# Attention with a router on one core: the place where token ranks are summed, the order of VectorE's work around the second scan, and idle products at the start

## The chip, the cores and the metric

One program on one core of one Trainium2 chip. The metric is device time in microseconds; runs of the same kernel are compared by their median. TensorE (PE) multiplies, VectorE (DVE), ScalarE (ACT) and GpSimd (POOL) do elementwise work, SyncE (SP) issues most of the transfers. Each engine works through its own queue in order.

## The reference

Gated linear attention (a recurrence over time) gives x; a cosine router sends each token to one of eight experts.

```python
# q, k, v, alpha: (4, 8, 768, 48); w1: (8, 384, 1024); w2: (8, 1024, 384)
for t in range(S):
    state = alpha[:, :, t, :, None] * state + np.einsum('bhd,bhe->bhde', k[:, :, t], v[:, :, t])
    y[:, :, t] = np.einsum('bhd,bhde->bhe', q[:, :, t], state)
x = y.transpose(0, 2, 1, 3).reshape(3072, 384)
logits = (x / norm(x)) @ (emb / norm(emb)).T / tau
e = argmax(logits); gate = softmax(logits)[e]
out = gate * (relu(x @ w1[e]) @ w2[e])
```

## The kernel before

The sequence is cut into 24 chunks of 128 tokens, six to each batch entry. One loop over `s` runs 28 iterations; iteration `s` does a different step for several chunks at once, so that every engine has work:

- `keys_back(s - 1)`: four transposes on PE (`pkb`), not for a batch entry's last chunk. They are the first products of an iteration, and their start is taken below as the iteration's start (`pa` where they are missing).
- `rows(s - 3)`: eight products that turn chunk `s - 3` into token rows with their router logits; VectorE sums the logits (`x`, L605), ScalarE copies the rows (L609).
- `decays(s)`: transposes of decays, keys and queries (`pa`, `pk`, `pq`, L416). VectorE scans `pa` backwards (`r`, L460), makes `kr` (L467), a reciprocal (`ini`, L470) and the second scan, forwards (`a`, L474). GpSimd multiplies the queries by `a` (`qs`, L479).
- `scores(s - 1)`: 16 records of products of `kr` and `qs` (`sc`, L540); VectorE masks one half (`sm`, L543), ScalarE copies the other and GpSimd masks it (L545).
- `mix_states(s - 2)` (L566), `update(s - 1)` (`pd`, L519, into the single bank of the pool `ps_mm`; VectorE adds `dec` to it and gives `state`, L527 or L529), `mix_chunk(s - 2)` (L579).

Every third chunk or so a group of tokens is complete (`GROUPS`). `choose(g)` then finds each token's expert on VectorE (`top`, `win`, `best`, `chosen`) and GpSimd adds the counts (`before`, L322, one addition for each chunk): in the program at the end of iterations 5, 8, 11, 14, 17, 20, 22 and later. One iteration on, in 6, 9, 12, 15, 18, 21, 23 and later, `place(g)` sums the ranks with two small products (L331, L335); VectorE makes row numbers of them (`at_row`, `row`, `dest`), and GpSimd sends one chunk of tokens to memory in each iteration (`xs`, L294), all that are left from iteration 21 on. GpSimd also copies token numbers into the next group's rows (`x` from `toks`, L603), which waits until the transfers out of that buffer have landed.

After the loop come the experts, eight in turn, with PE working throughout. The first expert's early part (`pxe`, `phe`) is in the last iterations, once its weights have come.

The code's order is not the final one: a scheduler lays out each engine's queue from the dependences, and `issue_after` holds an instruction back behind another. A pool's buffers are reused in turn, and a bank must be read before it is written again.

Of the kernel before, what the change touches and what calls it, by code (L numbers as in the profile page):

```python
# [9 lines left out]
FP32 = mybir.dt.float32  # L10
I32 = mybir.dt.int32
AF = mybir.ActivationFunctionType
ALU = mybir.AluOpType
# [14 lines left out]
def kernel(  # L28
# [12 lines left out]
    nc = tc.nc  # L41
    B, H, S, D = q.shape
    E, DM = expert_emb.shape
    F = w1.shape[2]
    P = 128
    DP = 64
    NP = H // 2
    NCH = S // P
    N = B * S
    NS = N // P  # L50
# [15 lines left out]
    S0, EARLY = 18, 2  # L66
# [117 lines left out]
    with ExitStack() as c1:  # L184
# [73 lines left out]
        def prepare_first(a0):  # L258

            p0 = ps_tr.tile([P, NP, NS], FP32, tag="tr", name="p0")  # L260
            for p in range(NP):
                nc.tensor.transpose(
                    p0[:, p], a0[:, 2 * p : 2 * p + 2].rearrange("s h d -> s (h d)"),
                    ident[:NS, :NS],
                )
            nc.vector.tensor_copy(al0, p0)
# [54 lines left out]
                eng = nc.vector if s == NS - 1 else nc.gpsimd  # L321
                eng.tensor_tensor(before[:, s + 1], before[:, s], chosen[:, s], ALU.add)  # L322

        def place(g, pyx):

            s0, s1 = GROUPS[g]
            n = s1 - s0
            ch = chosen[:, s0:s1]
            rkf = pyx[:, 0, RK : RK + n * E]
            rk = rkf.rearrange("p (s e) -> p s e", e=E)  # L330
            nc.tensor.matmul(  # L331
                rkf, lhsT=ones, rhs=before[:, s0:s1].rearrange("p s e -> p (s e)"),
                start=True, stop=False, skip_group_check=True,
            )
            nc.tensor.matmul(  # L335
                rkf, lhsT=earlier, rhs=ch.rearrange("p s e -> p (s e)"),
                start=False, stop=True, skip_group_check=True,
            )
            at = work.tile([P, GMAX, E], FP32, name="at_row")[:, 0:n]
            nc.vector.tensor_tensor(at, rk, ch, ALU.mult)  # L340
            row = work.tile([P, GMAX], FP32, name="row")[:, 0:n]
            nc.vector.tensor_reduce(row.unsqueeze(2), at, axis=AX.X, op=ALU.add)
            nc.vector.tensor_copy(dest[:, s0:s1], row)
            send.extend(range(s0, s1))
# [68 lines left out]
        def turned(t, name):  # L413
            pt = ps_tr.tile([P, NP * P], FP32, tag="tr", name=name)
            for p in range(NP):
                nc.tensor.transpose(  # L416
                    pt[:, p * P : (p + 1) * P],
                    t[:, 2 * p : 2 * p + 2].rearrange("p h d -> p (h d)"),
                    ident,
                )  # L420
            return pt
# [17 lines left out]
        def behind(s):  # L439

            queue = ExitStack()
            for call in st[s]["last"]:
                queue.enter_context(tc.issue_after(call.ins))
            return queue

        def decays(s):

            c = s % NCH
            d = st[s]
            i = s % NBUF
            L = NP * P
            pa = turned(at_s[i], "pa")
            r = r_s[s % NR]
            nc.vector.tensor_tensor_scan(  # L460
                r[:, L - 2 :: -1], pa[:, L - 1 : 0 : -1], inr[:, L - 2 :: -1],
                1.0, ALU.mult, ALU.add,
            )
            pk = turned(kt_s[i], "pk")
            d["kr"] = kr = work.tile([P, NP, P], FP32, name="kr", bufs=3)
            krf = kr.rearrange("p n t -> p (n t)")
            nc.vector.tensor_tensor(krf, pk, r, ALU.mult)  # L467
            rv = r.rearrange("p (n t) -> p n t", t=P)
            ini = ini_s[s % 2]
            nc.vector.reciprocal(  # L470
                ini.rearrange("p (n t) -> p n t", t=P)[:, :, 0:1], rv[:, :, 0:1]
            )
            a = work.tile([P, L], FP32, name="a")
            by_dve = nc.vector.tensor_tensor_scan(a, pa, ini, 0.0, ALU.mult, ALU.add)  # L474
            pq = turned(qt_s[i], "pq")
            d["qs"] = qs = work.tile([P, NP, P], FP32, name="qs", bufs=4)
            qc = work.tile([P, NP * P], FP32, name="qc")
            nc.scalar.copy(qc, pq)  # L478
            by_pool = nc.gpsimd.tensor_tensor(  # L479
                qs.rearrange("p n t -> p (n t)"), qc, a, ALU.mult  # L480
            )
            if c > 0:
                d["end"] = end = work.tile([P, NP, 1], FP32, name="end", bufs=3)
                nc.gpsimd.tensor_tensor(end, rv[:, :, 0:1], al0[:, :, s : s + 1], ALU.mult)
            d["last"] = by_dve, by_pool
# [22 lines left out]
        def update(s):  # L508

            c = s % NCH  # L510
            if c == NCH - 1:
                return
            d = st[s]
            kb, vt = d["kb"], vt_s[s % NBV]
            pd = ps_mm.tile([P, NP, DP], FP32, tag="mm", name="pd")
            for p in range(NP):
                for hh in range(2):
                    h = 2 * p + hh
                    nc.tensor.matmul(  # L519
                        pd[DP * hh : DP * hh + DP, p],  # L520
                        lhsT=kb[:, h * DP : (h + 1) * DP],
                        rhs=vt[:, h],
                        start=True, stop=True,
                    )
            carried["state"] = state = work.tile([P, NP, DP], FP32, name="state")
            if c == 0:
                nc.vector.tensor_copy(state, pd)  # L527
            else:
                nc.vector.tensor_tensor(state, pd, d["dec"], ALU.add)  # L529

        def scores(s):

# [18 lines left out]

        NQ = NP // 2
        YX = NQ * P
        RK = YX + NQ * (2 * D + E)

        def mix_states(s):
            d = st[s]
# [78 lines left out]
        def warm(n):  # L636

            pw = ps_mm.tile([P, P], FP32, tag="mm", name="pw")
            for _ in range(n):
                nc.tensor.matmul(pw, lhsT=ident, rhs=ident, start=True, stop=True)  # L640
# [8 lines left out]
        for s in range(NS + 4):  # L649
            if s + 2 <= NS:  # L650
                load(s + 2)
            if 0 <= s - 1 < NS:
                keys_back(s - 1)

            r = s - 4
            g = group_of[r] if r >= 0 else 0
            due = r >= 0 and r == GROUPS[g][1] - 1
            if 0 <= s - 3 < NS:
                rows(s - 3)
                if due:  # L660
                    place(g, st[s - 3]["pyx"])
            elif due:
                place(g, ps_y.tile([P, 2, 512], FP32, name="pyx"))
            if s < NS:
                decays(s)
            if s == 0:
                with behind(s):
                    prepare_first(a0)
                warm(2)
            if 0 <= s - 1 < NS:  # L670
                decay_state(s - 1)
                scores(s - 1)
# [1 line left out]
                mix_states(s - 2)  # L674
            if 0 <= s - 1 < NS:
                update(s - 1)
            if 0 <= s - 2 < NS:
                mix_chunk(s - 2)
            if s == 1:
# [14 lines left out]
                first_layer_early(0, 2)  # L694
            if s == NS + 1:
                first_layer_early(2, 4)
            if r == S0 - 1:
                first_expert()
            with behind(s) if s < NS else ExitStack():
                for c in send[:] if s >= S0 + 3 else send[:1]:  # L700
                    to_rows(dest[:, c : c + 1], x_g[group_of[c]][:, c - GROUPS[group_of[c]][0]])
# [266 lines left out]
```

## Time and profile before

| | us |
|---|---|
| median of 3 runs | 477.31 (474.83 to 478.24) |
| the profiled execution | 473.6 |
| its span, first to last instruction | 471.8 |

1.8 us of the profiled execution lie outside the span. PE is busy for 445.9 us of the span (95%) at a mean granted clock of 0.973; VectorE, ScalarE and GpSimd are busy for 37, 31 and 29%. Times in the trace are microseconds from the span's start. The granted clock is 1.00 at 2.4 GHz and 0.50 at 1.2 GHz. A busy figure for PE holds modelled ends, so an idle time is read from the waits, not from 100% less the busy share.

### The profile page before, as it was taken

The numbers are of one execution on the slowest core, as the hardware profiler recorded it, in microseconds if no ns is written. First come the engines' busy times: TensorE is split into PE (matmuls) and PEld (weight loads), VectorE is DVE, ScalarE is ACT, GpSimd is POOL, SyncE is SP. The second block draws the span as 40 slices with busy tenths as digits, with TensorE's granted clock in tenths as the row PEclk, the third lists the DMA queues.
The fourth block names the chain that finished last, engine by engine and source line by source line (L and its number), as shares of the span: only waits on it lengthen the run. The fifth ranks groups of instructions, "written<-read, shape, count | busy, mean of one in ns | idle before, by whom it ended". The sixth has DMA issues, their size and how long they took to land. (4 is left out here: it accounts for less than half of the span.)

```text
span 471.8 us, 8748 instructions
## 1 busy us (share of the span) xinstructions
PE 445.9 (95%) x3286; PEld 313.0 (66%) x3287; DVE 174.0 (37%) x467; ACT 147.5 (31%) x304; POOL 137.4 (29%) x231
## 2 busy tenths in 40 slices
PE   7899989998998998999999999999999999999993
PEld 6787878787887876676655655555656555655551
DVE  6787476785867752341221111111221121011010
ACT  3343334343334342373640330201650250210200
POOL 6356455655636642430101001010200101001001
PEclk9899889998989899999999999999999999999997
DMA  9999996885862396286702704501901800001000
GB/s 138 163 158 158 173 176 135 152 150 122 167 120 69 100 360 233 68 268 250 273 1 85 293 17 156 196 18 31 322 32 25 329 0 35 16 1 47 1 18 31
DMA packets 119362, 60.02 MB, mean 127 GB/s; under 512 B 102287, under 2 KB 113816, under 8 KB 119312
## 3 DMA queue, kind: packets, MB, share of 16 engines
q1 hardware_dynamic: 115208, 49.14, 44.4%
q0 software_dynamic: 3728, 10.16, 6.0%
q8 instruction: 32, 0.52, 0.5%
q14 instruction: 18, 0.15, 0.1%
q10 hardware_dynamic: 376, 0.05, 0.1%
HBM read 49.69 MB, written 11.45 MB: 130 GB/s over the span
## 5 line engine op out<-in xcount | busy, mean ns | idle before, releaser
L799 PE MATMUL ph<-xT,w 128*128 128x384 f32 (+1 forms) x384 | 119.4, 462 | 1.5 <-ACT hT L803 0.5
L810 PE MATMUL pyo<-w,hT 128*128 128x384 f32 x352 | 115.6, 488 | 0.0
L799 PEld LDWEIGHTS ph<-xT,w 128*128 128x128 f32 x384 | 67.7, 190 | 44.0 <-issue 5.2
L810 PEld LDWEIGHTS pyo<-w,hT 128*128 128x128 f32 x352 | 66.3, 190 | 45.3
L737 POOL DMA_INDIRECT out_dram<-y,sx x25 | 24.1, 965 | 232.0 <-DVE y L813 168.6
L803 ACT ACTIVATE hT<-ph 128x384 f32<-128x384 f32 (+1 forms) x64 | 29.1, 459 | 121.4 <-PE ph L799 121.3
L813 DVE TENSOR_SCALAR y<-pyo,gt 128x384 f32<-128x384 f32 x22 | 13.6, 618 | 108.9 <-PE pyo L810 108.9
L479 POOL TENSOR_TENSOR qs<-qc,a 128x512 f32<-128x512 f32 x24 | 30.5, 1272 | 40.7 <-DVE a L474 21.3
L753 DVE COPY xT<-pxg 128x384 f32<-128x384 f32 (+1 forms) x30 | 15.1, 503 | 66.6 <-PE pxg L752 63.6
L540 PE MATMUL sc<-qs,kr 64*128 64x128 f32 x384 | 31.4, 298 | 1.7 <-DVE en L277 1.5
L460 DVE TENSOR_TENSOR_SCAN r<-pa,inr 128x511 f32<-128x511 f32 x24 | 29.2, 1218 | 4.1 <-PE pa L416 4.1
L540 PEld LDWEIGHTS sc<-qs,kr 64*128 64x128 f32 x384 | 25.6, 196 | 6.4 <-issue 3.6
L474 DVE TENSOR_TENSOR_SCAN a<-pa,ini 128x512 f32<-128x512 f32 x24 | 29.4, 1224 | 1.2 <-DVE ini L470 0.5
L294 POOL DMA_INDIRECT xs<-x,dest x24 | 24.5, 1020 | 14.3 <-ACT ehT L633 5.1
L579 PE MATMUL pyx<-sm,vt 128*64 128x128 f32 x384 | 27.9, 292 | 0.0
L595 PE MATMUL pyx<-sel,yT 128*128 128x104 f32 x192 | 27.0, 284 | 0.2 <-ACT yT L585 0.2
L585 ACT COPY yT<-pyx 128x512 f32<-128x512 f32 x24 | 14.1, 586 | 39.0 <-PE pyx L579 39.0
L595 PEld LDWEIGHTS pyx<-sel,yT 128*128 128x128 f32 x192 | 23.6, 193 | 3.7 <-ACT yT L585 3.3
L579 PEld LDWEIGHTS pyx<-sm,vt 128*64 128x64 f32 x384 | 22.9, 149 | 0.9 <-issue 0.9
L762 ACT ACTIVATE gx<-xg 128x384 f32<-128x384 f32 x32 | 16.7, 522 | 15.8 <-DMA xg<-xs 14.7
L478 ACT COPY qc<-pq 128x512 f32<-128x512 f32 x24 | 14.0, 584 | 23.7 <-PE pq L416 23.3
L609 ACT COPY x<-pyx 128x384 f32<-128x384 f32 x24 | 11.6, 483 | 24.7 <-DVE x L605 24.7
(169 smaller groups left out, 514.7 us busy)
## 6 DMA issues: line engine op xcount, KB each, us to landing
w<-in_moe_w_dram SPq DMA_DIRECT2D x16, 1536.0 KB, 9.6
kt<-in_k_dram SPq DMA_DIRECT2D x24, 192.0 KB, 3.6
qt<-in_q_dram SPq DMA_DIRECT2D x24, 192.0 KB, 5.0
vt<-in_v_dram SPq DMA_DIRECT2D x24, 192.0 KB, 4.0
xg<-xs SPq DMA_DIRECT2D x22, 196.5 KB, 7.6
at<-in_alpha_dram SPq DMA_DIRECT2D x24, 168.0 KB, 4.8
xg<-xs SPq DMA_DIRECT2D x8, 98.2 KB
at<-in_alpha_dram SPq DMA_DIRECT2D x24, 22.5 KB, 4.3
```

Of the source, the lines that this page charges most:

```text
L294: ins = nc.gpsimd.indirect_dma_start(out=xs, out_offset=bass.IndirectOffsetOnAxis(ap=rows, axis=0), in_=x, in_offset=None, bounds_check=E ...
L460: nc.vector.tensor_tensor_scan(r[:, L - 2 :: -1], pa[:, L - 1 : 0 : -1], inr[:, L - 2 :: -1], 1.0, ALU.mult, ALU.add,)
L474: by_dve = nc.vector.tensor_tensor_scan(a, pa, ini, 0.0, ALU.mult, ALU.add)
L479: by_pool = nc.gpsimd.tensor_tensor(qs.rearrange("p n t -> p (n t)"), qc, a, ALU.mult)
L540: nc.tensor.matmul(sc[hh][:, p], lhsT=kr[sl, p], rhs=qs[sl, p], start=True, stop=True)
L579: nc.tensor.matmul(pyx[to : to + DP, hh, q * P : (q + 1) * P], lhsT=vt[:, 2 * p + hh], rhs=sm[hh][:, p], start=("dec" not in d and q == 0) ...
L595: nc.tensor.matmul(px[:, hh, q], lhsT=yT[:, hh, q], rhs=sel[:, hh, q], start=True, stop=True, skip_group_check=True,)
L737: ins = nc.gpsimd.indirect_dma_start(out=out, out_offset=bass.IndirectOffsetOnAxis(ap=col, axis=0), in_=y, in_offset=None, bounds_check=N - 1,
L762: nc.scalar.activation(x2, xg[:, t, 0:DM], AF.Square, accum_out=sq[:, t])
L799: nc.tensor.matmul(ph, lhsT=w1_t[:, i, f * P : (f + 1) * P], rhs=xT[:, i], start=(i == 0), stop=(i == KT - 1),)
L803: nc.scalar.activation(hT[:, f], ph, AF.Relu)
L810: nc.tensor.matmul(py, lhsT=hT[:, f], rhs=w2_t[:, f], start=(f == 0), stop=(f == FT - 1),)
```

## The change

Four edits:

- `place(g)` no longer writes into columns of the bank pair of `pyx`, which `rows` uses, but into a tile `rk` of the pool `ps_mm`, the one bank that `update` writes; and it is called near the end of the iteration, no longer right behind `rows`.
- `decays(s)` is split. Its second half, `decay_queries(s)` (reciprocal, second scan, `qs`, `end`), is called behind `update(s - 1)`, and held back on the queues until VectorE's state sum of chunk `s - 1` where there is one.
- `prepare_first` and its two idle products move with it, still in iteration 0.
- Five idle products (`warm(5)`, tile `pw`, in `ps_mm` too) are called in iteration 1.

On PE, the place of iteration 9 (names: `pyx` and `rk` written from `before` and `chosen` are the ranks; `pyx` from `sel` is `rows`). Before:

```order
L494 MATMUL pkb<-ident,kr 128x128 x4
L416 MATMUL pa<-ident,at_116 128x128 x2
L595 MATMUL pyx<-sel,yT 128x104 x4
L416 MATMUL pa<-ident,at_116 128x128 x2
L416 MATMUL pk<-ident,kt_124 128x128 x4
L416 MATMUL pq<-ident,qt_120 128x128
L331 MATMUL pyx<-before,ones 128x24
L335 MATMUL pyx<-chosen,earlier 128x24
L416 MATMUL pq<-ident,qt_120 128x128 x3
```

and now, from the update of that iteration to the scores of the next:

```order
L525 MATMUL pd<-vt_130,kb 64x64 x8
L584 MATMUL pyx<-sm_944,vt_129 64x128 x4
L584 MATMUL pyx<-sm_945,vt_129 64x128 x4
L331 MATMUL rk<-before,ones 128x24
L335 MATMUL rk<-chosen,earlier 128x24
L500 MATMUL pkb<-ident,kr 128x128 x4
L416 MATMUL pa<-ident,at_117 128x128
L600 MATMUL pyx<-sel,yT 128x104 x4
L416 MATMUL pa<-ident,at_117 128x128 x3
```

The rank products stood among the transposes of the same iteration and now stand behind its last products.

On VectorE, iteration 8, in which a group's experts are chosen. Before:

```order
L460 SCALAR_TENSOR_TENSOR r_134<-pa,inr 128x511
L312 TENSOR_REDUCE top<-x 128x3
L467 TENSOR_TENSOR kr<-pk,r_134 128x512
L470 RECIPROCAL ini_135<-r_134 128x4
L314 TENSOR_TENSOR win<-x,top 128x24
L474 SCALAR_TENSOR_TENSOR a<-pa,ini_135 128x512
L315 TENSOR_TENSOR win<-win,first 128x24
L317 TENSOR_REDUCE best<-win 128x3
L543 TENSOR_TENSOR sm_944<-sc_946,causal 128x512
L319 TENSOR_TENSOR chosen<-win,best 128x24
L529 TENSOR_TENSOR state<-pd,dec 128x256
```

and now:

```order
L459 SCALAR_TENSOR_TENSOR r_134<-pa,inr 128x511
L312 TENSOR_REDUCE top<-x 128x3
L466 TENSOR_TENSOR kr<-pk,r_134 128x512
L314 TENSOR_TENSOR win<-x,top 128x24
L315 TENSOR_TENSOR win<-win,first 128x24
L317 TENSOR_REDUCE best<-win 128x3
L319 TENSOR_TENSOR chosen<-win,best 128x24
L549 TENSOR_TENSOR sm_944<-sc_946,causal 128x512
L535 TENSOR_TENSOR state<-pd,dec 128x256
L479 RECIPROCAL ini_135<-r_134 128x4
L483 SCALAR_TENSOR_TENSOR a<-pa,ini_135 128x512
```

The second scan `a` stood ahead of the mask and the state sum and is now the last of them; `chosen` comes ahead of the mask.

On GpSimd, from the query product of iteration 8 to that of iteration 9. Before:

```order
L479 TENSOR_TENSOR qs<-qc,a 128x512
L688 MEMSET xg_91 128x393
L294 DMA xs<-x,dest 25024x393
L545 AFFINE_SELECT sm_945<-sm_945 128x512
L322 TENSOR_TENSOR before<-before,chosen 128x8
L504 TENSOR_TENSOR dec<-state,end 128x256
L322 TENSOR_TENSOR before<-before,chosen 128x8 x2
L603 COPY x<-toks 128x3
L484 TENSOR_TENSOR end<-r_132,al_139 128x4
L479 TENSOR_TENSOR qs<-qc,a 128x512
```

and now:

```order
L485 TENSOR_TENSOR qs<-qc,a 128x512
L692 MEMSET xg_91 128x393
L294 DMA xs<-x,dest 25024x393
L490 TENSOR_TENSOR end<-r_132,al_139 128x4
L608 COPY x<-toks 128x3
L551 AFFINE_SELECT sm_1046<-sm_1046 128x512
L510 TENSOR_TENSOR dec<-state,end 128x256
L485 TENSOR_TENSOR qs<-qc,a 128x512
```

The count's additions are no longer in this stretch (they now stand ahead of the query product of iteration 8), and the copy of token numbers now stands ahead of a mask and of `dec`.

The diff:

```diff
-        def place(g, pyx):
+        def place(g):
...
-            rkf = pyx[:, 0, RK : RK + n * E]
-            rk = rkf.rearrange("p (s e) -> p s e", e=E)
+            rk = ps_mm.tile([P, GMAX, E], FP32, tag="mm", name="rk")[:, 0:n]
+            rkf = rk.rearrange("p s e -> p (s e)")
             nc.tensor.matmul(
                 rkf, lhsT=ones, rhs=before[:, s0:s1].rearrange("p s e -> p (s e)"),
-                start=True, stop=False, skip_group_check=True,
+                start=True, stop=False,
             )
...
             nc.vector.tensor_tensor(krf, pk, r, ALU.mult)
+            pq = turned(qt_s[i], "pq")
+            d["qc"] = qc = work.tile([P, NP * P], FP32, name="qc")
+            nc.scalar.copy(qc, pq)
+            d["a"] = pa, r
+
+        def decay_queries(s):
+            c = s % NCH
+            d = st[s]
+            L = NP * P
+            pa, r = d["a"]
             rv = r.rearrange("p (n t) -> p n t", t=P)
...
             by_dve = nc.vector.tensor_tensor_scan(a, pa, ini, 0.0, ALU.mult, ALU.add)
-            pq = turned(qt_s[i], "pq")
             d["qs"] = qs = work.tile([P, NP, P], FP32, name="qs", bufs=4)
-            qc = work.tile([P, NP * P], FP32, name="qc")
-            nc.scalar.copy(qc, pq)
...
             if c == 0:
-                nc.vector.tensor_copy(state, pd)
+                d["sum"] = nc.vector.tensor_copy(state, pd)
             else:
-                nc.vector.tensor_tensor(state, pd, d["dec"], ALU.add)
+                d["sum"] = nc.vector.tensor_tensor(state, pd, d["dec"], ALU.add)
...
-
-            r = s - 4
-            g = group_of[r] if r >= 0 else 0
-            due = r >= 0 and r == GROUPS[g][1] - 1
             if 0 <= s - 3 < NS:
                 rows(s - 3)
-                if due:
-                    place(g, st[s - 3]["pyx"])
-            elif due:
-                place(g, ps_y.tile([P, 2, 512], FP32, name="pyx"))
             if s < NS:
                 decays(s)
-            if s == 0:
-                with behind(s):
-                    prepare_first(a0)
-                warm(2)
             if 0 <= s - 1 < NS:
                 decay_state(s - 1)
                 scores(s - 1)
...
             if 0 <= s - 1 < NS:
                 update(s - 1)
+            if s < NS:
+
+                done = st[s - 1].get("sum") if s > 1 else None
+                with tc.issue_after(done.ins) if done is not None else ExitStack():
+                    decay_queries(s)
+            if s == 0:
+                with behind(s):
+                    prepare_first(a0)
+                warm(2)
+            if s == 1:
+                warm(5)
             if 0 <= s - 2 < NS:
                 mix_chunk(s - 2)
...
-            if r == S0 - 1:
-                first_expert()
+
+            r = s - 4
+            if r >= 0:
+                g = group_of[r]
+                if r == GROUPS[g][1] - 1:
+                    place(g)
+                    if r == S0 - 1:
+                        first_expert()
```

## Rows read from the trace of the kernel before

**Rows 1.** The page: busy time of each engine, and PE's granted clock by slices.

```profile
PE 445.9 (95%) x3286; PEld 313.0 (66%) x3287; DVE 174.0 (37%) x467; ACT 147.5 (31%) x304; POOL 137.4 (29%) x231
PEclk9899889998989899999999999999999999999997
```

**Rows 2.** What PE waited for: us in total, times, longest.

```profile
PE pyx L331 <- POOL before L322: 6.9, 4, 1.9
PE pyx L331 <- ACT x L609: 3.7, 4, 1.4
...
PE sc L540 <- DVE en L277: 1.5, 1, 1.5
```

**Rows 3.** Stretches: busy us by engine (PE, PEld, DVE, ACT, POOL), clock, DMA, GB/s.

```profile
16.24:19.65 3.41, 3.41 (x18) 3.37 (x18) 1.41 (x2) 0.59 (x1) 0.00 (x0) 0.52 1.20 156
40.91:169.94 129.03, 119.43 (x1508) 103.08 (x1507) 89.68 (x189) 48.83 (x88) 73.81 (x122) 0.93 0.73 144
...
67.44:70.85 3.41, 3.41 (x50) 2.85 (x50) 2.35 (x6) 1.08 (x2) 1.86 (x4) 0.52 0.73 117
...
152.77:156.18 3.41, 3.41 (x50) 3.01 (x48) 2.01 (x3) 0.58 (x1) 2.11 (x2) 0.52 0.02 5
```

**Rows 4.** Timeline of PE: start, duration, instruction, idle time before and its releaser.

```profile
66.26 0.40 PE L331 MATMUL pyx<-before,ones 128*128 128x24 f32 x2 [1.93 <-POOL before L322]
...
88.74 0.37 PE L331 MATMUL pyx<-before,ones 128*128 128x24 f32 x2 [1.08 <-ACT x L609]
...
91.53 0.65 PE L494 MATMUL pkb<-ident,kr 128*128 128x128 f32 x4
...
97.68 0.66 PE L494 MATMUL pkb<-ident,kr 128*128 128x128 f32 x4
...
103.24 0.66 PE L494 MATMUL pkb<-ident,kr 128*128 128x128 f32 x4
...
180.29 0.40 PE L331 MATMUL pyx<-before,ones 128*128 128x16 f32 x2 [1.50 <-POOL before L322]
```

**Rows 5.** Timeline of all engines: the steps from scores to the next scores.

```profile
94.50 1.16 PE L540 MATMUL sc<-qs,kr 64*128 64x128 f32 x16
...
96.19 0.69 PE L519 MATMUL pd<-vt,kb 128*64 128x64 f32 x16
...
101.21 0.69 DVE L467 TENSOR_TENSOR kr<-pk,r 128x512 f32<-128x512 f32 x1
...
101.82 0.17 DVE L470 RECIPROCAL ini<-r 128x4 f32<-128x4 f32 x1
...
102.10 1.22 DVE L474 TENSOR_TENSOR_SCAN a<-pa,ini 128x512 f32<-128x512 f32 x1
...
103.46 1.27 POOL L479 TENSOR_TENSOR qs<-qc,a 128x512 f32<-128x512 f32 x1 [1.58 <-DVE win L315]
103.53 0.68 DVE L543 TENSOR_TENSOR sm<-sc,causal 128x512 f32<-128x512 f32 x1
...
104.70 0.41 DVE L529 TENSOR_TENSOR state<-pd,dec 128x256 f32<-128x256 f32 x1
```

**Rows 6.** Source of L319: duration ns min/median/max of `chosen`.

```profile
L319 DVE TENSOR_TENSOR chosen<-win,best x10: 158/656/957, 41.1 to 188.0; 128x24 f32<-128x24 f32 x6, 128x16 f32<-128x16 f32 x2, 128x8 f32<-128x8 f32 x2
```

**Rows 7.** Timeline of POOL: sends of token rows, and the copies that wait for them.

```profile
63.64 1.02 POOL L294 DMA_INDIRECT xs<-x,dest  x1 [0.16 <-DVE state L529]
67.92 0.19 POOL L603 COPY x<-toks 128x3 f32<-128x3 f32 x1 [1.43 <-DMA xs<-x,dest]
...
158.49 0.97 POOL L294 DMA_INDIRECT xs<-x,dest  x1 [0.30 <-DMA xs<-x,dest]
161.62 0.19 POOL L603 COPY x<-toks 128x1 f32<-128x1 f32 x1 [1.52 <-issue]
```

**Rows 8.** Timeline of the start: the two idle products, and iteration 3.

```profile
7.46 0.61 PE L640 MATMUL pw<-ident 128*128 128x128 f32 x4
...
26.58 0.67 PE L566 MATMUL pyx<-qs,dec 64*64 64x128 f32 x16 [0.45 <-ACT x L609]
```

More of the change, by code (lines that the diff above doesn't have):

```diff
@@ L336, in place @@
                 rkf, lhsT=earlier, rhs=ch.rearrange("p s e -> p (s e)"),
-                start=False, stop=True, skip_group_check=True,
+                start=False, stop=True,
             )
@@ L446, in decays @@
         def decays(s):
-            c = s % NCH
             d = st[s]
@@ L474, in decays @@
             by_dve = nc.vector.tensor_tensor_scan(a, pa, ini, 0.0, ALU.mult, ALU.add)
-            pq = turned(qt_s[i], "pq")
             d["qs"] = qs = work.tile([P, NP, P], FP32, name="qs", bufs=4)
-            qc = work.tile([P, NP * P], FP32, name="qc")
-            nc.scalar.copy(qc, pq)
             by_pool = nc.gpsimd.tensor_tensor(
-                qs.rearrange("p n t -> p (n t)"), qc, a, ALU.mult
+                qs.rearrange("p n t -> p (n t)"), d["qc"], a, ALU.mult
             )
@@ L553 @@
         YX = NQ * P
-        RK = YX + NQ * (2 * D + E)
         def mix_states(s):
```

## The prediction

> **What bounds the kernel now.** I read the page first: PE is busy 95% of the span, and its clock line is below 9 only at the ends, with a row of eights among the first third of the slices [rows 1]. So PE sets the time, and what can be won is where PE waits or runs at the lower clock. The table of PE's waits is short: 6.9 us for the count's additions on GpSimd and 3.7 us for ScalarE's copy of the rows, all of it ahead of the rank products of L331, then 1.5 us once at the start [rows 2]. The timeline shows what such a wait is: at 66.26 the rank product stands in the middle of the transposes and waits 1.93 us for the last addition, at 88.74 it waits 1.08 us for ScalarE, which has to finish reading the bank pair that the ranks are written into [rows 4]. Third, the clock by stretches: six stretches of 3.41 us run at 1.2 GHz (three of them shown), PE busy all the time in each [rows 3]. The first, at 16.24, comes close behind the wait at the start, and each of the other five begins at most 2 us behind a rank product that had waited (67.44 behind 66.26); the wait at 88.74 has none behind it [rows 3, 4]. The rest of the loop is PE back to back: undisturbed iterations take 6.15 us (91.53 to 97.68) or, where there is no `mix_states`, 5.55 us (97.68 to 103.24) [rows 4].
>
> **What the change removes.** The rank products go behind `mix_chunk`, and the additions on GpSimd are ahead of the query product one iteration earlier, so neither the additions nor ScalarE's copy can be late for them: 6.9 + 3.7 = 10.6 us of waits go, 1.5 of them in the tail at 180.29 [rows 2, 4]. With the waits I let the five half-clock stretches behind them go: a stretch of 3.41 us at half speed holds 1.7 us of work, so 5 x 1.7 = 8.5 us [rows 3]. Together 19.1 us. A check from the other side: iterations 6 to 23 take 129.0 us [rows 3]; eighteen of 6.15 us would be 110.7, so 18.3 us are disturbance and the rank products themselves (seven times some 0.45 us, 3.2 in all). That leaves 15.1, and 1.8 more for the three iterations of 5.55 us: 16.9, against 17.6 by terms without the tail. The rank products cost the same in their new place and are no term.
>
> **What the new bank asks.** The ranks now wait until VectorE has read `pd` out of that bank. From the scores' start to the end of `pd` are 2.38 us (94.50 to 96.88), the state sum takes 0.41 [rows 5], so with a hand-over it ends some 2.9 us behind the scores' start; `mix_chunk` is about 1 us of products between. The scores start 2.97 us into an iteration (91.53 to 94.50 [rows 4, 5]), so the sum is done at 5.85 and the ranks are due at 6.15. Nothing, and the work that hides it is `mix_chunk`. The next `update` needs the bank 4.6 us later; `at_row` reads it long before.
>
> **The second scan behind the state sum.** Now the reciprocal and scan follow the sum. From the scores' start: 2.38 to the end of `pd`, 0.41 sum, 0.28 from the reciprocal's start to the scan's (101.82 to 102.10), 1.22 scan, 0.14 to GpSimd (103.32 to 103.46), 1.27 query product, and 0.1, an estimate from that 0.14, for each of the two other hand-overs: 5.90 us [rows 5]. That is a loop, from one iteration's scores to the next one's, and it must stay under 6.15. It does by 0.25, so plain iterations cost nothing: before, this work lay beside PE with far more room. What waits behind the held scan on VectorE is small: the next logits' sum and first scan are not due before 2.2 us of the next iteration.
>
> In a choosing iteration four dependent small steps of 0.2 us come between `kr` (ends 4.22 us into the iteration, 101.90 less 97.68 [rows 4, 5]) and the mask, which then ends at about 5.5, the sum at 5.9, the scan at 7.3, `qs` at 8.7. Where the iteration is 5.55 us, the next scores are due at 5.55 + 2.97 = 8.52: 0.2 us late in iterations 8, 14 and 20, together 0.6. Where `chosen` takes its median 0.656 us and not its shortest 0.158 [rows 6], it is 0.5 more each, 2.1 together. I take the short one, because the long ones run beside GpSimd's `qs`, and now GpSimd stands waiting for `chosen`. The Trainium skill, SBUF — State Buffer, section "Who interferes with whom", says that a VectorE instruction with two SBUF inputs contends with a GpSimd instruction that reads SBUF; it speaks for the short value.
>
> **GpSimd's queue.** The copy of token numbers now stands ahead of a mask, `dec` and `qs`, in iterations 9 and 15, and it waits for the send just ahead of it: 4.28 us from send to copy (63.64 to 67.92), 3.13 at the fastest (158.49 to 161.62) [rows 7]. The send begins about 3.7 us into the iteration (behind the late `qs` of the iteration before and a memset), so the copy ends at about 7.9, and 0.65 mask, 0.6 `dec` and 1.27 `qs` end at 10.4; scores are due at 6.15 + 0.45 + 0.2 + 2.97 = 9.8. 0.7 us each, 1.4 together; from 0 (3.1 us landing) to 2.0. In iteration 12 and 18 the copy is behind `qs` and costs nothing. In iteration 22 three sends go one behind the other and the copy waits for the third: it starts some 8.1 us into the iteration, `qs` ends at 10.8, scores are due at 9.1: 1.7 us, and with most of a half-clock stretch behind it (1.5) 3.2; from 0 to 3.4. By the fit in the Trainium skill, DMA: Bandwidth & Descriptors, section "Anatomy of one DMA — SWDGE (gpsimd) path" (2.0 us and bytes over 436 GB/s), a send of 128 rows of 1572 B would be an estimated 2.5 us, the two waits of 0.7 would vanish and the third be 1.1; the traced 3.1 to 4.3 decide, and with the page the time would be about 2 us lower.
>
> **The start.** Two idle products take 0.61 us [rows 8], so five some 1.4; they can only follow the state copy out of their bank, so they stand behind the wait of 1.5 us, not in it. They fill some of the gaps there; I take 0.7 net, from 0 to 1.4, and leave the first half-clock stretch as it is. In iteration 3 the routing constants on GpSimd now follow a later `qs`, and VectorE's casts, then the logits' sum, then ScalarE's copy wait for them. PE waited 0.45 us there [rows 8]; the second scan's shift of some 2 us makes it about 1.4: 0.9 more, and half a chance of a half-clock stretch, 0.8. Start: 2.4, from 0.6 to 3.3. SP's queue keeps its order; its early fetch and weights hang on iteration 21's sends, which go later by what the ranks do, against a PE that comes sooner. I take nothing, up to 2.
>
> **Sum.** 19.1 less 0.6, 1.4, 3.2 and 2.4 is 11.5 us. Against the profiled execution, 473.6 us (span 471.8 and 1.8 outside), that is 462.1. The median of the runs is 3.7 higher; how often the clock falls may differ from run to run, and the changed kernel has fewer occasions, so I add nothing for it: **462.0 us**.
>
> **Rivals.** *The waits move into the scores.* `qs` is late in every place cycle: `chosen` long (1.5 more), landings of 4.3 us and more (0.6), and behind four of the seven new waits a half-clock stretch (6.8): 462 + 8.9 = 471. For it speaks that the loop has only 0.25 us of room; against it that the wait of 1.08 us at 88.74 had no half clock behind it, and the new ones are shorter. *The half clock isn't the waits' doing.* Then only waits go, and none of the charged stretches comes either: 10.6 less 5.3, 468.3. For: one wait without a stretch; against: every stretch follows a wait closely. *Slower.* The scan's loop becomes the bound: if hand-overs add 0.55 us to its 5.90, each of some 17 full iterations is 0.3 longer (5 us) and PE idles in each, so the clock falls at least as often as before (8.5): 475.5; at 1.05 us more, 17 x 0.8 and the clock give 484. It decides at 6.15; against it every hand-over in the sum is a traced one. *The edits cancel*: rank waits only turn into waits for the bank or the query product of the same length: 474 to 478.
>
> **Numbers.** My forecast 0.60 (455 to 466), waits in the scores 0.18, clock not the waits' 0.10, cancel 0.07, slower 0.05. Range 455 to 471: the first three but for the upper end of the second. A measurement of this kernel tells 1%, 4.8 us, from nothing: faster means under 472.5. Faster 0.85, within 1% 0.10, slower 0.05.
>
> **What would show it.** No wait of `rk` for `before` or `x`; one or two half-clock stretches between 40 and 160, not five; `sc` waiting for `qs` under 1 us in iterations 10 and 16 and some 1.7 in 23; iteration starts 6.15 apart elsewhere. I am wrong if plain iterations are longer than 6.2 us or if half-clock stretches stay without waits ahead of them.

## The result, and the profile after

The changed kernel takes 463.48 us (median of 4 runs, 462.27 to 465.06) where the kernel before, on the same chip, took 477.59 (474.83 to 478.24): ratio 0.972, 95% interval 0.967 to 0.977, so 14 us less. On another chip, in the last group of experiments, before took 471.95 and the changed kernel 464.91, ratio 0.985 (0.982 to 0.988), 7 us less: it is before that differs between the chips. The profiled execution after took 465.06 us (span 463.4); that of before had a span of 471.8, so the two profiles have to explain 8.4 us.

The page, for comparison with [rows 1]: PE's busy time fell by 6.8 us, and its clock line has three slices of eight ahead of the end where before had six.

```profile
PE 439.1 (95%) x3296; PEld 309.8 (67%) x3297; DVE 172.5 (37%) x467; ACT 147.5 (32%) x304; POOL 138.1 (30%) x231
...
PEclk9899999998999999998999999999999999999998
```

What PE waited for in the changed kernel (total, times, longest). No wait of the rank products is left of [rows 2]. Three rows are new or have grown: the scores for `qs` (0.2 us before), `hT_half` in the experts, and `mix_states` for ScalarE's row copy (0.7 us before).

```profile
PE sc L546 <- POOL qs L485: 5.2, 4, 2.4
PE pyo L849 <- ACT hT_half L841: 2.5, 1, 2.5
PE pyx L571 <- ACT x L614: 2.1, 3, 0.7
...
PE sc L546 <- DVE en L277: 1.6, 1, 1.6
```

Stretches of the changed kernel (columns as in [rows 3]): iterations 6 to 23 (without the rank products at the end of 23), then the two half-clock stretches behind the start (before had five), then iteration 6 to the last product ahead of the experts (`tot`), and the experts.

```profile
41.53:160.00 118.47, 110.92 (x1505) 96.53 (x1503) 86.66 (x184) 48.65 (x87) 73.15 (x120) 0.99 0.77 150
111.08:114.49 3.41, 3.41 (x50) 2.85 (x48) 0.69 (x1) 0.59 (x1) 1.89 (x3) 0.50 0.38 85
210.06:213.48 3.42, 3.09 (x10) 2.37 (x12) 0.00 (x0) 0.55 (x2) 0.00 (x0) 0.50 0.99 404
...
41.53:180.95 139.42, 131.33 (x1678) 114.32 (x1676) 93.64 (x215) 56.53 (x105) 81.26 (x131) 0.99 0.78 174
180.95:463.40 282.45, 271.21 (x1196) 163.60 (x1196) 48.85 (x177) 75.26 (x172) 34.90 (x36) 0.99 0.30 104
```

The last two pieces before:

```profile
40.91:192.43 151.52, 140.12 (x1679) 120.32 (x1677) 94.51 (x215) 56.07 (x104) 81.41 (x134) 0.94 0.72 160
192.43:471.80 279.37, 270.19 (x1198) 161.89 (x1197) 49.13 (x178) 75.79 (x173) 34.81 (x36) 0.99 0.30 105
```

So the start is 0.6 us longer, the loop and its tail 12.1 shorter, and the experts, in which no line was changed, 3.1 us longer in this execution. In a second execution of the changed kernel (e3_changed below) the experts take 279.49 us, so these 3.1 us are not the change's own.

The timeline of PE, to be held against [rows 4]. At 65.75 the rank product follows the chunk's products with no wait; a plain iteration is still 6.15 us (74.60 to 80.75), one without `mix_states` 5.55 (93.17 to 98.72). The scores wait in iterations 10 and 16, `mix_states` in iterations 6, 12 and 18, and far behind, in the experts, the half block's second layer.

```profile
65.75 0.40 PE L331 MATMUL rk<-before,ones 128*128 128x24 f32 x2
...
71.42 1.16 PE L546 MATMUL sc<-qs,kr 64*128 64x128 f32 x16 [2.38 <-POOL qs L485]
...
74.60 0.66 PE L500 MATMUL pkb<-ident,kr 128*128 128x128 f32 x4
...
85.15 0.67 PE L571 MATMUL pyx<-qs,dec 64*64 64x128 f32 x16 [0.70 <-ACT x L614]
...
93.17 0.66 PE L500 MATMUL pkb<-ident,kr 128*128 128x128 f32 x4
...
98.72 0.66 PE L500 MATMUL pkb<-ident,kr 128*128 128x128 f32 x4
...
110.60 1.67 PE L546 MATMUL sc<-qs,kr 64*128 64x128 f32 x16 [2.33 <-POOL qs L485]
...
210.39 4.45 PE L849 MATMUL pyo<-w,hT_half 128*64 128x384 f32 x16 [2.47 <-ACT hT_half L841]
```

GpSimd's timeline says why the scores wait at 71.42 (its counterpart is the first pair of [rows 7]). The query product of iteration 8 is issued 0.34 us behind its scan and ends as the scores of iteration 9 (62.58) begin: no room. Then the send, then the copy of token numbers, which stands 4.47 us for that send, and behind it the mask, `dec` and the query product of iteration 9, for which the scores of iteration 10 wait.

```profile
61.25 1.28 POOL L485 TENSOR_TENSOR qs<-qc,a 128x512 f32<-128x512 f32 x1 [0.34 <-DVE a L483]
...
63.04 1.02 POOL L294 DMA_INDIRECT xs<-x,dest  x1 [0.16 <-issue]
...
68.79 0.19 POOL L608 COPY x<-toks 128x3 f32<-128x3 f32 x1 [4.47 <-DMA xs<-x,dest]
68.92 0.64 POOL L551 TENSOR_SCALAR_AFFINE_SELECT sm<-sm 128x512 f32<-128x512 f32 x1
69.53 0.62 POOL L510 TENSOR_TENSOR dec<-state,end 128x256 f32<-128x256 f32 x1
70.10 1.27 POOL L485 TENSOR_TENSOR qs<-qc,a 128x512 f32<-128x512 f32 x1
```

ScalarE's timeline in the experts says why PE waits at 210.39: the squares of the next expert's rows stand ahead of `hT_half` in its queue, and wait 6.95 us for those rows, whose fetch is queued behind that expert's weights.

```profile
208.65 0.52 ACT L772 ACTIVATE gx<-xg 128x384 f32<-128x384 f32 x1 [6.95 <-DMA xg<-xs]
...
209.95 0.66 ACT L841 ACTIVATE hT_half<-ph 128x256 f32<-128x256 f32 x2
```

### The profile page after: what moved, and what is told of

Same layout as the page of the kernel before. It is cut to its first block, busy times and chain, and to the rows that moved or that the text cites. A ratio compares the mean times of both kernels' runs of the same rounds, so it can differ in the third digit from the quotient of the medians.

```text
span 463.4 us, 8702 instructions
## 1 busy us (share of the span) xinstructions
PE 439.1 (95%) x3296; PEld 309.8 (67%) x3297; DVE 172.5 (37%) x467; ACT 147.5 (32%) x304; POOL 138.1 (30%) x231
## 5 line engine op out<-in xcount | busy, mean ns | idle before, releaser
L546 PE MATMUL sc<-qs,kr 64*128 64x128 f32 x384 | 28.9, 289 | 6.9 <-POOL qs L485 5.2
L546 PEld LDWEIGHTS sc<-qs,kr 64*128 64x128 f32 x384 | 24.0, 190 | 11.5 <-POOL qs L485 9.3
L584 PE MATMUL pyx<-sm,vt 128*64 128x128 f32 x384 | 26.0, 276 | 0.3 <-issue 0.3
L584 PEld LDWEIGHTS pyx<-sm,vt 128*64 128x64 f32 x384 | 21.0, 138 | 1.9 <-issue 1.9
L550 ACT COPY sm<-sc 128x512 f32<-128x512 f32 x24 | 14.1, 588 | 17.8 <-PE sc L546 17.8
```

The lines of the kernel that those rows point to most:

```text
L546: nc.tensor.matmul(sc[hh][:, p], lhsT=kr[sl, p], rhs=qs[sl, p], start=True, stop=True)
L584: nc.tensor.matmul(pyx[to : to + DP, hh, q * P : (q + 1) * P], lhsT=vt[:, 2 * p + hh], rhs=sm[hh][:, p], start=("dec" not in d and q == 0) ...
```

## The experiments

Times are medians, ratios are to before on the same chip (472.95 us for the first four, 472.23 for the next four, 471.95 for the last three). Theory: the rank products' new place takes out the waits and most half-clock stretches; the scan's shift and what rides on it give some of it back. Rivals: the shift is what frees the ranks; the waits only move; the clock falls for another reason.

**The ranks' move alone** (e1_place_only): the changed kernel with the scan where it was before, and no idle products. The diff is against the changed kernel.

```diff
                 decays(s)
+                decay_queries(s)
...
-                done = st[s - 1].get("sum") if s > 1 else None
-                with tc.issue_after(done.ins) if done is not None else ExitStack():
-                    decay_queries(s)
...
-            if s == 1:
-                warm(5)
```

> The ranks in the bank of the state's update, behind mix_chunk; the second scan stays ahead of VectorE's mask and state sum as before, and the five idle products are left out. Theory (the move of the rank products carries the gain; the scan's shift and the idle products are near neutral): no wait of rk for before or x, at most two half-clock stretches between 40 and 160, no 2.4 us waits of the scores for qs, since the query product is issued with 2 us of room again; 458 to 465 us. Rival (the scan's shift is needed, since scan and reciprocal ahead of the state sum let the rank products wait for the bank and GpSimd's additions behind the query product): waits of about 1 us at most of the seven places with half-clock stretches behind them, 468 us or more.

455.41 us, ratio 0.962 (0.957 to 0.966): 17.5 us less than before, below the 458 to 465 expected, and 8.3 us less than the nearest kernel to the whole change on this chip (e1_no_warm, 463.72). Its page and table of waits:

```profile
PEclk9999999999999999999999999999999999999998
```

```profile
PE pyx L571 <- ACT x L614: 3.8, 4, 1.2
...
PE rk L331 <- DVE state L535: 1.5, 4, 0.4
```

No wait for qs, and no half-clock stretch before the end. The rank products do wait for the state sum here, 0.4 us four times, as the rival said, but not for 1 us. GpSimd's timeline holds the same send and copy as that of the changed kernel, and a wait of the copy that costs nothing: the copy comes 4.49 us behind the send, `qs` ends at 66.41, and PE's scores begin at 68.12. With the scan in its old place the query product has 1.7 us of room.

```profile
60.34 1.02 POOL L294 DMA_INDIRECT xs<-x,dest  x1
...
64.83 0.19 POOL L608 COPY x<-toks 128x3 f32<-128x3 f32 x1 [1.65 <-DMA xs<-x,dest]
...
65.13 1.28 POOL L485 TENSOR_TENSOR qs<-qc,a 128x512 f32<-128x512 f32 x1
```

**The scan's shift alone** (e1_scan_only): before, with the second scan held behind the state sum; the ranks stay where they were.

```diff
+        def decay_queries(s):
...
                 update(s - 1)
+            if s < NS:
+                done = st[s - 1].get("sum") if s > 1 else None
+                with tc.issue_after(done.ins) if done is not None else ExitStack():
+                    decay_queries(s)
```

> The second scan behind the state sum as in the changed kernel; the rank products stay in the bank pair of the rows at their old place, and no five idle products. Theory (the rank products' place is what cost): rank waits stay, though GpSimd's additions now go ahead of the query product, so that the 6.9 us for before shrink and the 3.7 us for ScalarE's row copy stay; with the score waits behind the token copy on top 470 to 478 us. Rival (the scan's shift alone takes the waits away, since the additions stand ahead of the query product): no rank wait over 0.3 us, 466 us or less.

463.63 us, ratio 0.978 (0.974 to 0.982). Both sides missed: I had 470 or more, the rival no rank wait over 0.3. The waits for `before` are gone altogether, because GpSimd now adds the counts ahead of the query product, and the waits for ScalarE shrink to at most 0.9; the scores wait instead, up to 1.1 us.

```profile
PE pyx L331 <- ACT x L615: 3.3, 6, 0.9
PE sc L546 <- POOL qs L485: 2.8, 5, 1.1
```

So either half of the change removes the waits for `before`; those for ScalarE's copy the scan's shift leaves almost whole (3.3 of 3.7 us). Alone they bring 17.5 and 9.3 us; together (7 and 14 on two chips) no more than the first does by itself.

**Without the idle products** (e1_no_warm): the changed kernel less one line.

```diff
-            if s == 1:
-                warm(5)
```

> The changed kernel without the five idle products behind the first chunk's state. Theory: they were costed at 0.7 us net; the changed kernel comes to its third iteration 1.7 us later than before, so without them 0.5 to 1.5 us less, 462 to 463 us. Rival: they keep the clock up in the start; without them one more half-clock stretch, 464 to 466 us.

463.72 us, ratio 0.977 (0.973 to 0.982), between the two ratios of the changed kernel: no difference that can be told. In its trace iteration 6 begins 0.4 us earlier (41.14 against 41.53), and the half-clock stretch in the start is there with and without them.

**The token copy later** (e1_copy_late): the changed kernel, its copy behind the query product of the iteration that first needs the buffer.

```diff
-                nc.gpsimd.tensor_copy(x_g[g][:, :, TK], toks[:, s0:s1])
...
+            if 0 <= s - 3 < NS and s - 3 == GROUPS[group_of[s - 3]][0]:
+                g = group_of[s - 3]
+                with behind(s) if s < NS else ExitStack():
+                    nc.gpsimd.tensor_copy(x_g[g][:, :, TK], toks[:, GROUPS[g][0] : GROUPS[g][1]])
```

> The changed kernel with GpSimd's copy of token numbers held behind the query product of the iteration that first needs it, by which time the sends of the buffer's last group have landed. Theory (the two waits of 2.4 and 2.3 us of the scores for qs, and the half-clock stretch at 111.08, come from that copy standing ahead of mask, dec and qs while a send lands): both waits and the stretch go, 4.7 + 1.7 = 6.4 us less at the end of the loop, and 3 to 6.4 us less at the end of the program, 457 to 460 us. Rival (qs is late anyway, through the scan's loop in the 5.55 us iterations): the waits stay over 1 us, and the time moves by less than 2 us.

456.76 us, ratio 0.965 (0.961 to 0.970): as the theory had it, a little under its 457 to 460, and 7.0 us less than e1_no_warm (463.72), the nearest kernel with the copy in its old place on this chip. The two long waits are gone (5.2 us of waits for qs became 0.2), and the copy stands where it delays nothing:

```profile
65.45 1.27 POOL L485 TENSOR_TENSOR qs<-qc,a 128x512 f32<-128x512 f32 x1 [0.66 <-DVE at_row L340]
66.67 0.19 POOL L691 COPY x<-toks 128x3 f32<-128x3 f32 x1
```

New is one wait of 2.6 us at 158.80 for the early weights of the first expert, with a half-clock stretch that begins in it.

**Idle products in the old rank waits** (e2_fill): before, with six products ahead of the ranks.

```diff
                 if due:
+                    warm(6)
                     place(g, st[s - 3]["pyx"])
             elif due:
+                warm(6)
                 place(g, ps_y.tile([P, 2, 512], FP32, name="pyx"))
```

> The kernel before, with six idle products of 128 columns (about 1.8 us at full clock) ahead of the rank products at each of the places, so that PE is busy while the count's additions or the row copy are waited for. Theory (the half-clock stretches are the waits' doing): the idle products run inside the waits of 1 to 1.9 us, the stretches between 40 and 160 go from five to at most one, and the time falls by 4 to 8 us, to 466 to 470 where before runs at 473, though nothing of the waits themselves is gained. Rival (the stretches have another cause, such as the narrow rank products or power drawn by the loop): four or five stretches stay, and the time is that of before or up to 5 us more.

480.01 us, ratio 1.016 (1.012 to 1.020): 7.8 us slower, so the expected time was wrong, though the stretches went, as the theory forecast. The idle products are written into the bank of the state's update, so they wait for the state sum, 9.5 us in seven waits, and run behind the wait, not in it. That adds seven times some 1.8 us of work to waits that stay nearly as long as they were (10.6 us before).

```profile
62.86 0.49 PE L640 MATMUL pw<-ident 128*128 128x128 f32 x2 [1.27 <-DVE state L529]
...
64.06 1.30 PE L640 MATMUL pw<-ident 128*128 128x128 f32 x10
65.57 0.40 PE L331 MATMUL pyx<-before,ones 128*128 128x24 f32 x2 [0.21 <-POOL before L322]
```

```profile
PEclk9899999999999999999999999999999999999998
```

Yet with those waits there is no half-clock stretch between 40 us and the end of the work. So a wait of 1.2 to 1.8 us alone does not bring one. What else it takes, the products around it or the moment at which it falls, this run doesn't show.

**Rows ahead of weights** (e2_fetch_first): the changed kernel, in the experts' loop.

```diff
-                weights(i + 2)
                 to_rows(pads[:, i + 2 : i + 3], blank)
                 fetch(i + 2)
+                weights(i + 2)
```

> The changed kernel; in the experts' loop the rows of expert i+2 are fetched ahead of its weights, not behind them. Theory (of the loop's gain 3.1 us are given back at 210, where PE waits 2.5 us for hT_half behind ScalarE's gx, which waits for the fetched rows that land behind the weights, and a half-clock stretch of 1.7 us follows): gx no longer waits 7 us, the wait and the stretch go, 3 to 4 us less than the changed kernel (0.9717 of before becomes some 0.964). Rival (PE waits for the weights instead, which now land later, or the experts are bound by transfers anyway): the same time within 1 us.

464.23 us, ratio 0.983 (0.979 to 0.987): no gain in the total. In the experts the wait for `hT_half` is gone, no half-clock stretch stands there, and from `tot` (181.99) to the end (462.5) are 280.5 us, 1.9 less than 282.45, with 1.4 us of new waits for ScalarE's `hT`. But this doesn't bear the theory out: in e3_changed, with the fetch in its old place, the experts take 279.49 us (182.61 to 462.1), `hT_half` costs 0.2 us and no half-clock stretch stands there either. The wait at 210 was that one execution's, and no gain of the fetch order is shown. Also, in this execution the copy behind three sends was late in iteration 22, and the scores waited as long as in no other run, with a stretch of 6.83 us at 1.2 GHz from 154.85 on:

```profile
155.33 2.08 PE L546 MATMUL sc<-qs,kr 64*128 64x128 f32 x16 [3.14 <-POOL qs L485]
```

**The logits' sum ahead of the second scan** (e2_rows_first, and again as e3_place_rows): on top of e1_place_only.

```diff
+                reduced = st[s - 3].get("sum_x") if s >= 3 else None
+                with tc.issue_after(reduced.ins) if reduced is not None else ExitStack():
                     decay_queries(s)
```

> The kernel with the rank products moved and nothing else (e1_place_only), with VectorE's sum of the logits held ahead of the second scan, so that ScalarE's row copy can start sooner in the iterations without a state product. Theory (mix_states waits 3.8 us in four such iterations for the row copy, which waits for that sum, which stands behind the second scan): 2.5 to 3.8 us less, 0.9615 of before becomes 0.954 to 0.957. Rival (ScalarE's copy of the queries then takes the row copy's place, or the loop is bound elsewhere): less than 1 us.

453.71 us, ratio 0.960 (0.957 to 0.964), where e1_place_only had 0.9615: the waits of `mix_states` for the row copy fell from 3.8 to 0.4 us, but the medians by 1.7 us only, and the two intervals overlap. In the two traces, iteration 6 to `tot` takes 2.8 us less (131.49 against 134.26), as the theory has it; but iteration 6 begins 2.5 us later, with two half-clock stretches in the start that e1_place_only's trace has not.

**Both** (e2_both), by the last two diffs together:

> The kernel of e2_rows_first with the fetch order of e2_fetch_first. Theory: where the rows come in time already (no wait for hT_half in e1_place_only), the fetch order gains nothing more by itself, but with the loop shorter again the rows come late again, so 0 to 3 us less than e2_rows_first. Rival: the weights, now behind the rows, come late: 1 to 3 us more.

454.30 us, ratio 0.962 (0.958 to 0.965): the same as e2_rows_first. Where rows come in time the fetch order is worth nothing.

**The changed kernel again, and its parts held apart**, on one chip (e3_changed, e3_held_apart, e3_place_rows). The second is the whole change with the copy late and the scan held behind the logits' sum:

```diff
                 done = st[s - 1].get("sum") if s > 1 else None
+                reduced = st[s - 3].get("sum_x") if s >= 3 else None
+                with ExitStack() as held:
+                    for call in (done, reduced):
+                        if call is not None:
+                            held.enter_context(tc.issue_after(call.ins))
+                    decay_queries(s)
```

> The changed kernel as it is, on the same chip as the two beside it. Theory (what separates it from the variants is its queues, not the chip): 0.970 to 0.978 of before, with waits of the scores of 2 us or more again behind the token copy, in two or three places. Rival (the spread between chips and runs made the 8 us between it and the kernel with the place move alone): within 3 us of the two others.

> The changed kernel with all its parts, its token copy on GpSimd held behind the query product (as in e1_copy_late) and the second scan held behind VectorE's sum of the logits too (as in e2_rows_first). Theory (the scan's shift costs nothing by itself; what it cost was the copy that came ahead of a query product with no room left, and the logits' sum behind the scan): no waits of the scores or of mix_states over 0.5 us in the loop, the same as the other variant within 1.5 us, 0.957 to 0.963 of before. Rival (the shift costs by itself, since the loop from scores to scores has only 0.25 us of room): 2 us or more above it, with waits for qs in the choosing iterations.

> The rank products moved, the scan in its old place behind the logits' sum, no idle products (the kernel of e2_rows_first), on the same chip. Theory: 0.957 to 0.963 of before, as it ran before. Rival (its gain was the chip's): over 0.966.

464.91 us, ratio 0.985 (0.982 to 0.988); 452.56, ratio 0.958 (0.956 to 0.960); 453.25, ratio 0.960 (0.958 to 0.963). The waits of the first, then of the second:

```profile
PE sc L546 <- POOL qs L485: 8.0, 5, 2.6
PE pyx L571 <- ACT x L614: 2.1, 3, 0.7
```

```profile
PE phe L633 <- DMA w<-in_moe_w_dram: 1.4, 1, 1.4
...
PE sc L546 <- POOL qs L485: 0.3, 1, 0.3
```

The theory stands: with the copy and the logits' sum out of its way, the shifted scan costs nothing that can be measured, and the whole change so mended is 12.4 us below the change as it was made, on the same chip, and level with the ranks' move alone with the sum held ahead (452.56 and 453.25, with intervals that overlap). The long waits of the changed kernel came again, three of them (2.62, 2.49 and 2.45 us). Its ratio missed the expected 0.970 to 0.978, though its own time moved by 1.4 us only: before is 5.6 us faster on this chip.

## Why the prediction came out right, step by step

The time was right to 1.5 us (462.0 against 463.48), and the direction. That it came so close is luck. The terms were off in both directions, and the two profiles differ by 8.4 us where the sum has 11.5. Half of the rest was made up by chance: the forecast counts from the profiled execution of before, and the changed kernel's median lies 1.6 us below its own profiled execution. Against the two profiles, in us:

| step | predicted | traces |
|---|---|---|
| rank waits gone | -10.6 | -10.6 |
| half-clock stretches in the loop, at 1.7 each | -8.5 (five) | -6.8 (five became one) |
| ranks wait for the state sum | 0 | 0 |
| scores late in choosing iterations | +0.6 | 0 |
| scores late in 10 and 16, behind the copy | +1.4 | +4.7 |
| scores late in 23, with half clock | +3.2 | 0 |
| scores late once in the tail | - | +0.3 |
| start | +2.4 | +0.6 |
| `mix_states` late in 6, 12, 18, for the copy that the ranks had waited for | - | +2.1 |
| experts | 0, up to +2 | +3.1 (+0.1 in e3_changed) |
| sum | -11.5 | -6.6 |

The spans differ by 8.4; the other 1.8 us is busy time of PE in the loop that I could not tie to an instruction.

**What is removed.** Right for the ranks, and the ranks' move alone shows that their place is enough: 17.5 us less, where the step had 19.1 (a total, with waits of its own in it). The step missed two things. The waits for `before` were paid for twice, since the scan's shift by itself takes them out. And of the 3.7 us for ScalarE's copy 3.55 stood in iterations 6, 12 and 18 (1.08, 1.08 and 1.39), where the ranks were not the only ones to wait for it: `mix_states` writes the same bank pair, the only one of its pool, and PE comes to it right behind the scores. With the ranks gone it waits 2.1 us for the same copy in the same three iterations, so the waits fell by 8.5 us net. The copy is late there because the second scan goes ahead of the logits' sum on VectorE. It did so before, too, so this isn't the shift's doing; in iteration 12 before:

```profile
86.78 1.22 DVE L474 TENSOR_TENSOR_SCAN a<-pa,ini 128x512 f32<-128x512 f32 x1
87.92 0.17 DVE L605 TENSOR_REDUCE x<-pyx 128x8 f32<-128x32 f32 x1
```

The kernels with the sum held ahead of the scan bear this out: where the scan is in its old place (e2_rows_first) the waits of `mix_states` fall from 3.8 to 0.4 us, and with the shifted scan (e3_held_apart) from 2.1 to 0.2.

The check from the other side (16.9 against 17.6) agreed by chance. It counted the three iterations without `mix_states` as shorter, but not 6, 12 and 18, which have no `keys_back` and no `update`: iteration 12 takes 6.49 us now (80.75 to 87.24), with 0.70 of wait and some 0.46 of rank products, so 5.33 without them. With three of these the check gives 19.4, some 1.8 us more than the terms. That is the size of what is left over above, but nothing here ties the two together.

**The clock.** That the waits have to do with the stretches is borne out as far as it goes. In all these traces, each stretch between the start and the last one at the program's end begins inside a wait or within 2.3 us behind one: for example 111.08 behind 110.60 and 210.06 inside the wait that ends at 210.39 here, 71.92 and 157.26 behind waits of 2.62 and 2.45 in e3_changed, 45.64 and 86.60 behind rank waits of 0.92 and 0.93 at 43.63 and 84.42 in e1_scan_only. And e1_place_only and e3_held_apart, which have no wait over 1.1 us left in the loop, have none in it. But a wait is not enough. The prediction counted one without a stretch, at 88.74; [rows 4] shows a second, 1.50 us at 180.29. Nor did a third one of 0.93 in e1_scan_only draw one, nor the seven of e2_fill. And the changed kernel's two executions differ at the same places: here the wait of 2.38 us in iteration 10 drew none and that of 2.33 in iteration 16 drew one, in e3_changed 2.62 in iteration 10 drew one and 2.49 in iteration 16 none:

```profile
70.32 1.16 PE L546 MATMUL sc<-qs,kr 64*128 64x128 f32 x16 [2.62 <-POOL qs L485]
71.92:75.33 3.41, 3.41 (x43) 2.96 (x36) 2.02 (x4) 0.58 (x2) 1.61 (x4) 0.50 1.35 207
```

So neither the length of a wait nor the products around it settle it alone; what does stays open. 8.5 was a fair size, not a mechanism.

**The copy behind the send** is the step that failed by size. Its working was right in every part but one: the scores fell due 9.56 us into iteration 9 (9.8 predicted), the send began 3.56 into it (3.7), but from send to copy were 5.75 us, not 4.28; so the wait was 2.38 and not 0.7. In iteration 16 it was 5.69 and 2.33. The bound of 2.0 for both together was too low, since I took 4.28 [rows 7] for the long end; the loop before has nothing longer than 4.30 at this place, only its tail has 7.37 (171.93 to 179.30). The estimate of 2.5 us from the Trainium skill (DMA: Bandwidth & Descriptors, section "Anatomy of one DMA — SWDGE (gpsimd) path"), by which these waits would have vanished, was further off still; the changed kernel's trace has 2.98 to 5.75 from send to copy in the loop, and 7.43 in the tail.

**Three sends in iteration 22** is the same term, on the other side. In this execution the scores began just as `qs` ended (156.81 and 156.76), because PE had itself lost about 1.2 us in iteration 22 to gaps that the profile puts down to no wait. In three other executions the predicted wait came: 3.14 us (e2_fetch_first) and 2.45 us (e3_changed), each with a half-clock stretch, and 1.20 us (e1_no_warm) with none. The term is real and varies from run to run.

**The scan's loop.** The bound held: plain iterations stayed at 6.15. The loop is even shorter than the 5.90 of the sum, 5.61 us from the scores at 71.42 to the query product's end at 77.03. The choice of the short `chosen` was right. It was made from the trace, with the Trainium skill (SBUF — State Buffer, section "Who interferes with whom") beside it, and in the changed kernel's trace the median fell from the 656 ns of [rows 6] to 182, with GpSimd standing still for it in six of the ten places:

```profile
L319 DVE TENSOR_TENSOR chosen<-win,best x10: 167/182/274, 40.2 to 176.0; 128x24 f32<-128x24 f32 x6, 128x16 f32<-128x16 f32 x2, 128x8 f32<-128x8 f32 x2
```

**The start** cost a quarter of what I gave it: iteration 3 had no wait of 1.4 us, and the idle products some 0.4.

**The experts.** "Early fetch and weights ... nothing, up to 2" was about the wrong transfer. The early ones came in time; the rows of the second expert did not in this execution: PE was 11.5 us ahead at `tot`, the fetch that follows the weights only 9.7 (issued 197.80 against 207.49). But PE's lead isn't the whole cause: in e1_place_only it is 18 us ahead at `tot` (174.25), and nothing waits for `hT_half`; in e3_changed the wait is 0.2 us. What delayed the rows in this execution stays open.

## What to carry to other kernels

When a change moves work on an engine closer to its deadline, look at what else stands in that engine's queue ahead of the deadline and waits for a transfer: the copy of token numbers had waited 0.4 to 1.5 us in the loop without harm, and became a 2.4 us wait of PE when the query product lost its room (1.7 us in e1_place_only). When something stops waiting, ask who else waits for the same release: ScalarE's copy held up the rank products before and `mix_states` now. Run each half of a change alone before keeping both: here either took out the waits for `before`, and one of them alone was better than the two together. For a wait on a transfer, take the slowest landing in the trace, and more, for the bound, not the one beside the place.

## What was unexpected of the hardware

The sends that landed late share a mark. In the changed kernel, in the 3.86 us from the send at 63.04 in which 59 of its 64 packets begin, the queues' table has one transfer of kind "instruction", of 16 KB, which held a DMA engine for 1.4 us; in the stretch of the send at 83.71, whose copy came 4.29 us later, there is none in the first 3.3 us, in which 47 of its 64 packets begin.

```profile
q1 hardware_dynamic: 3085, 0.58, 113.9%
q0 software_dynamic: 59, 0.19, 17.5%
q8 instruction: 1, 0.02, 2.3%
```

The same holds of the send at 102.27 (5.69 us, one such transfer in its stretch). That code being fetched keeps a few of the send's packets waiting is argued from this, not shown: no run here moved the one against the other. Two sends of other runs speak against it as the only cause. In e1_no_warm the send at 124.33 took 5.36 us to its copy, with no such transfer in the 4.27 us in which 62 of its 64 packets begin; the loads' queue (q1) was at 111.2% there, as it was high (113.9%) above. In e2_both one overlapped the send at 59.45, and the copy came after 4.44 us. The load of the other transfers is a rival that stays untested.
